# A weight loaded in three pieces, and the last transposes of a GLA and MLP-mixer kernel moved from TensorE to the DMA crossbar

## The chip, the cores and the metric

The kernel runs on one core of one Trainium2 chip. The metric is the device time of one execution in microseconds (us). The core has five engines that run their own instruction streams side by side: TensorE (matrix multiplies and transposes; PE in the profile, its weight loads PEld), VectorE (DVE), ScalarE (ACT), GpSimd (POOL) and SyncE (SP). SP computes nothing here; its queue issues every DMA of the kernel. The 16 DMA engines that move the data are shared by all transfers.

## The reference

Two stages follow each other, for four batches of 768 tokens. The first is a gated linear attention with 8 heads of 48, the second an MLP mixer over 384 channels.

```
for t in range(S):                                  # 768 tokens, per batch and head
    state = alpha[t] * state + outer(k[t], v[t])    # 48 x 48
    y[t] = q[t] @ state
x = y as [batch, token, 8 * 48]

h  = relu(x.T @ w_tok1) @ w_tok2                    # mixes tokens, 768 -> 256 -> 768
u  = x + h.T
h2 = relu(u @ w_ch1) @ w_ch2                        # mixes channels, 384 -> 1536 -> 384
out = u + h2
```

All inputs and the output are float32 in DRAM; the kernel multiplies in bf16.

## The kernel before

**Tiling.** A batch is cut into six chunks of 128 tokens, numbered through all batches (chunk 18 is the first of batch 3). The recurrence over tokens becomes matrix products inside a chunk and a 48 x 48 state per head handed from chunk to chunk.

**One chunk of attention.** Four loads bring alpha, k, q, v (`load`). ACT takes the logarithm of alpha (`la`, L243), TensorE sums it over the tokens (`cum`, L352), ACT exponentiates the sums with either sign (`ek`, `eq`, L256 and L258). POOL multiplies k and q by them (`pkk`, `pkq`, L275, one 128 x 384 product each; for batch 0 the q product is on DVE) and casts v (`vb`, L282). Keys and queries must then have channels on the partitions: TensorE transposes both in pieces of 64 x 64 into two PSUM banks (`tr`, through `row_tiles`, L289), and ACT or DVE copies the two banks to SBUF (`tp`, L297, into `tkq`). From there come the chunk's score matrix (`gt`, L387), its masking (`gm`, L309, DVE), the state (`state`, `st`, `ss`) and the output (`y`, then `x`, L333). The chunks of batches 0 and part of 1 are worked off in pairs by `paired_chunks`, with the same steps.

**The mixer of one batch.** `tok1` (L602) and `ht` (relu) mix the tokens down, `tok2` (L651) mixes them up again, and DVE adds x to give u (`u`, L657, one per chunk). u is transposed as well: `utp` (L667, again `row_tiles`) handles three chunks at a time (part 0 is chunks 0 to 2, part 1 chunks 3 to 5 of the batch) and `ut` (L669) copies two banks to SBUF. Batch 0 gets its transposed u by other matmuls (`mixed`, `xt` and `uT`). Then `ch1` (L691) has 24 groups of three matmuls, one for each of 12 blocks of 128 hidden channels and each half of the tokens; a group for half 0 reads only part 0 of the transposed u. ACT or DVE applies the relu (`rt`). `ch2` (L715) multiplies back, in three groups of four matmuls for each chunk (batch 3's last chunk in two column ranges), DVE adds u (`o`, L728), and SP stores the result (`out`, L731).

**Weights.** `weight` (L735) loads each weight in pieces into a staging tile and casts it to bf16 there. The first channel weight (`m0`, `m1`, 384 x 768 each) comes through the staging tile `rt_late`; each piece has three casts of 128 x 768 (the `cast` of L756). `ch1` finds the piece of a block by its column (`divmod(mc * 128, WP)`).

**Order.** Nothing is scheduled at run time. The calls of `g.add` number the operations, and the string `ORDER` lists these numbers in the order in which they are emitted; each engine works off its own operations in that order and waits where an input or a buffer isn't ready. A letter behind a number picks the engine (A, D, P), the digits behind a point the PSUM banks. An item `f2` is a fill: a matmul of zeros into bank 2 (L792) that keeps TensorE running where it would wait. The costs at `g.add` (`{"PE": 0.25}`, `dma=`) belong to the planner that wrote the order; at run time they do nothing but name the engine.

All loads and stores stand in one sequence on SP's queue. Input tiles have eight slots, so loads run ahead of the work by up to eight chunks. The last load is chunk 23's v; only stores come behind it.

Of the kernel before, what the change touches and what calls it, by code (L numbers as in the profile page):

```python
# [25 lines left out]
0 1 f0 2 f0 f0 f0 f0 f0 3 f0 f0 f0 f0 f0 4 28 f0 29 f0 f0 30.0 5 31.1 32 f2 f2 38 6 f2 35 f2 33 f2 f2 f2 39 f2 34 f2  # L26
36 40 f2 43.2 41 7 f3 66 47.3 f4 65 48 44 49A 50D f4 67.4 46A 45D 68.5 69 f6 51.67 75 72 54.01 8 70 52 f3 f3 76 f3 73
f3 77 f3 80.3 78 f2 9 84.2 56 f6 85 105 81 71 f6 104 87D f6 f6 10 86A f6 f6 83D 106.6 82A 55 107.5 108 53 91.14 11 114
88.23 92 f0 42P 37A f0 f0 109 90 f0 58.07 115 89 57.13 60A 93 f2 116 12 f2 f2 59 f2 f2 f2 112 f2 111 63 61 117 14
123.2 64A f0 62 f0 124 74A 79P 119.0 110 16 120 125D 126A f4 94.41 122A 121D 18 96 127.57 97 130.36 95.20 128 113A  # L30
118P 100 132 98 102 133.4 99A 20 131 13P f5 103A 169.5 101 163.6 24 166.2 f3 15P 129 141.3 135 142.0 143 136 134.17
17P 137 139 145 138D 147 140A 144 146 259 148 150 149 151 19D 152 172.4 178.1 162A 161D 175.7 f0 173 176 174A 167 177D
260 164 168A 170 22D 21P 165A 179 f0 171A 23D f0 261 f0 180A f0 189.0 201.3 190A 195.4 262 202A 181.7 27D 25P 196A
185.2 26D 182A 153 193.6 186A 211.5 264 194D 223.1 263 212D 227.0 224A 265.3 228A 266.4 155 267 217.7 273 270 207.2
274 209.6 268 300 208D 218A 276 213.5 210D 215.1 214A 269 187.0 301 271 216A 203.4 188A 219.3 275 204A 302 225.2 220A
154D 199.7 272 226A 278.65 277 279 200A 303 221.1 280D 281A 156P 183.0 222A 282 283 184A 292.43 284D 285A 197.2 304
294 286.71 157 305 198D 289.05 205.6 287 306.4 288 206A 159 191.2 308 291 307.7 309 311 239.6 296 314 343 290 315
# [41 lines left out]
class Graph:  # L79
# [5 lines left out]
    def add(self, name, costs, emit, reads=(), writes=(), prio=0, dma=None, new=(), tail=0.0, rows=False, loose=False, n=0, late=0.0):  # L85
        self.ops.append(Op(costs, emit, new))
        return self.ops[-1]
# [6 lines left out]
def kernel(  # L94
# [12 lines left out]
    nc = tc.nc  # L107
    B, H, S, D = q.shape
    C = 128
# [725 lines left out]
```

## Time and profile before

| what | value |
|---|---|
| time, median of 3 runs | 174.1 us (174.01 to 174.3) |
| the profiled execution | 174.24 us |
| its span in the trace | 172.5 us |
| DMA, mean over the span | 30.20 MB, 175 GB/s |
| first matmul of ch1, batch 0 | 33.1 us |
| first matmul of ch1, batch 3 | 146.3 us |

A row of a group reads: line, engine, operation, output<-inputs by the program's names, shape, xcount, then the busy time in all and the mean of one in ns, then how long the engine sat idle just before and what ended that. A row of the chain or of the timeline begins with the start in the span and a length in us; in the timeline, rows of one kind that follow each other closely are merged and the counts added. A row of a stretch of time gives its bounds, its length and each engine's busy time with the number of instructions. Matmuls overlap in the pipeline: one of 128 x 384 is listed with 326 ns, and they follow each other every 0.16 us.

### The profile page before, as it was taken

Reading aid. Unit: us, or ns where it says so; the run is one execution under the profiler, and the core shown is the slowest. Engines: PE = TensorE matmul, PEld = TensorE weight load, DVE = VectorE, ACT = ScalarE, POOL = GpSimd, SP = SyncE. Lnnn points to the kernel's source line nnn. Section 1 sums busy time; section 2 is a strip of 40 time slices with the busy share of each in tenths; the row PEclk is TensorE's granted clock in tenths of the full one; section 3 lists DMA queues with packets and bytes.
Section 4 is the critical chain, followed back from the end, with each engine's and each line's share of the span. In section 5 each row is a group of like instructions: output and inputs, shape, how many; then the busy total and the mean of one; then the engine's idle time right before and its main releaser. Section 6 shows DMA issues by size and latency. Waiting matters only on the chain.

```text
span 172.5 us, 5143 instructions
## 1 busy us (share of the span) xinstructions
PE 166.5 (96%) x2099; PEld 106.8 (62%) x2099; DVE 102.0 (59%) x212; ACT 96.0 (56%) x206; POOL 72.3 (42%) x114
## 2 busy tenths in 40 slices
PE   7999979999999999999999999999999999999993
PEld 3566656665666567566666665666676656656562
DVE  3159977544653597689593727495988248132231
ACT  2577552699865655497887231699771112865000
POOL 7252542319485782944877111499941000000000
PEclk9999999999999999999999999999999999999999
DMA  5999999999998999999999999995000221100133
GB/s 134 261 261 265 232 335 398 309 234 337 256 307 168 205 254 219 225 170 198 165 204 151 196 219 223 211 210 92 4 4 0 79 104 50 46 4 0 46 115 113
DMA packets 86150, 30.20 MB, mean 175 GB/s; under 512 B 79600, under 2 KB 85104, under 8 KB 86128
## 3 DMA queue, kind: packets, MB, share of 16 engines
q1 hardware_dynamic: 86128, 29.89, 75.2%
q8 instruction: 16, 0.26, 0.7%
q14 instruction: 6, 0.05, 0.1%
HBM read 25.17 MB, written 4.72 MB: 173 GB/s over the span
## 4 chain that ended last, share of the span: by engine, by line
PE 78%; DVE 6%; POOL 4%; DMA 3%; issue 3%; ACT 2%; SPq 1%; DVEq 0%; POOLq 0%
PE bank L691 27%; PE bank L715 23%; PE bank L289 4%; PE bank L651 3%; DMA ina<-in_alpha_dram 3%; PE bank L602 3%; DVE gm L309 2%; PE bank L387 2%; PE bank L338 2%; PE bank L423 2%; POOL pkk L275 2%; PE bank L521 1%; PE bank L411 1%; PE bank L352 1%; SPq L205 1%
## 5 line engine op out<-in xcount | busy, mean ns | idle before, releaser
L691 PE MATMUL bank<-ut,wc 128*128 128x384 bf16 x288 | 51.1, 326 | 0.0
L691 PEld LDWEIGHTS <-wc 128*128 128x128 bf16 x288 | 26.6, 98 | 16.5
L275 POOL TENSOR_TENSOR pkk<-ink,ek 128x384 bf16<-128x384 f32 x24 | 24.3, 1022 | 17.7 <-ACT ek L256 14.9
L715 PE MATMUL bank<-wc,rt 128*128 128x384 bf16 x144 | 26.5, 326 | 0.0
L715 PE MATMUL bank<-wc,rt_late 128*128 128x384 bf16 (+2 forms) x156 | 25.1, 314 | 0.0
L728 DVE TENSOR_TENSOR o<-bank,x 128x384 f32<-128x384 f32 (+2 forms) x19 | 10.1, 536 | 18.2 <-PE bank L715 18.2
L589 ACT ACTIVATE rt<-bank 128x384 bf16<-128x384 f32 x33 | 16.3, 494 | 7.4 <-PE bank L691 7.0
L282 POOL CAST vb<-inv 128x384 bf16<-128x384 f32 x21 | 10.5, 506 | 22.3 <-DMA inv<-in_v_dram 17.6
L715 PEld LDWEIGHTS <-rt_late 128*128 128x128 bf16 x156 | 14.4, 98 | 8.2
L275 POOL TENSOR_TENSOR pkq<-inq,eq 128x384 bf16<-128x384 f32 x18 | 17.9, 1003 | 2.8 <-ACT eq L258 2.8
L589 ACT ACTIVATE rt_late<-bank 128x384 bf16<-128x384 f32 x33 | 16.1, 495 | 5.3 <-PE bank L691 5.3
L309 DVE TENSOR_TENSOR gm<-bank,u 128x512 bf16<-128x512 f32 x28 | 17.3, 682 | 2.8 <-PE bank L387 2.6
L243 ACT ACTIVATE la<-ina 128x384 bf16<-128x384 f32 x24 | 12.1, 526 | 10.8 <-DMA ina<-in_alpha_dram 10.8
L715 PEld LDWEIGHTS <-rt 128*128 128x128 bf16 x144 | 13.2, 98 | 7.7
L792 PE MATMUL bank<-zeros 128*128 128x384 bf16 x61 | 15.1, 372 | 1.4 <-DVE la L192 1.2
L591 DVE TENSOR_SCALAR rt_late<-bank 128x384 bf16<-128x384 f32 x15 | 8.3, 554 | 10.0 <-PE bank L691 8.3
L309 DVE TENSOR_TENSOR gm<-bank,pmask 128x512 bf16<-128x512 f32 x20 | 12.7, 682 | 1.4 <-PE bank L521 1.3
L256 ACT ACTIVATE ek<-bank 128x384 f32<-128x384 f32 x24 | 11.4, 498 | 3.5 <-PE bank L355 2.0
L333 ACT CAST x<-bank 128x384 bf16<-128x384 f32 x16 | 7.3, 483 | 10.6 <-PE bank L338 9.4
L322 POOL TENSOR_TENSOR ss<-st,al 128x384 bf16<-128x384 f32 x12 | 10.0, 832 | 7.4 <-DVE st L319 5.4
L591 DVE TENSOR_SCALAR rt<-bank 128x384 bf16<-128x384 f32 x15 | 7.9, 554 | 5.3 <-PE bank L691 5.3
L297 ACT COPY tkq<-bank 128x512 bf16<-128x512 bf16 x17 | 9.3, 602 | 2.8 <-PE bank L289 2.7
(118 smaller groups left out, 237.3 us busy)
## 6 DMA issues: line engine op xcount, KB each, us to landing
out_dram<-o SPq DMA_DIRECT2D x23, 192.0 KB, 2.6
ina<-in_alpha_dram SPq DMA_DIRECT2D x14, 192.0 KB, 4.3
ink<-in_k_dram SPq DMA_DIRECT2D x14, 192.0 KB, 4.6
inq<-in_q_dram SPq DMA_DIRECT2D x14, 192.0 KB, 4.5
inv<-in_v_dram SPq DMA_DIRECT2D x14, 192.0 KB, 4.4
rt_late<-in_moe_w_ch_dram SPq DMA_DIRECT2D x2, 1152.0 KB, 10.1
rt_late<-in_moe_w_ch_dram SPq DMA_DIRECT2D x4, 576.0 KB, 7.1
ina<-in_alpha_dram SPq DMA_DIRECT2D x5, 384.0 KB, 6.3
```

Source lines behind the costliest of these rows:

```text
L243: g.add("la", {"ACT": 0.43}, lambda e: act.activation(la[:, :, 0:D], t, AF.Ln), key, [u["la"][1]], pr + 5)
L256: g.add("ek", {"ACT": 0.38}, lambda e: act.activation(ek, banks[bank.place][:, 0:HD], AF.Exp, scale=-1.0), [bank], [kek], pr + 4)
L275: lambda e, dst=dst, src=src, ex=ex: {"POOL": gps, "DVE": dve}[e].tensor_tensor(dst[:, :, 0:D], src, ex().rearrange("p (h d) -> p h d", h= ...
L282: lambda e: evict[e](vb, src), ksrc, [u["vb"][1]], pr + 4)
L309: g.add("gm", {"DVE": 0.60}, lambda e: dve.tensor_tensor(gm, banks[bank.place].rearrange("p (j t) -> p j t", j=4), wide(mask, [[0, 4], lis ...
L322: g.add("ss", {"POOL": 0.79}, lambda e: gps.tensor_tensor(ss, st.rearrange("p (h d) -> p h d", h=H), wide(al, [[1, 8], [0, D]]), ALU.mult) ...
L589: act.activation(dst, src, AF.Relu)
L591: dve.tensor_scalar_max(dst, src, 0.0)
L691: pe.matmul(banks[bank.place][:, 0:HD], lhsT=wc1[wp][:, kc, off : off + 128], rhs=ut_t[b % 2][:, kc, cs], start=(kc == 0), stop=(kc == NM ...
L715: pe.matmul(banks[bank.place][:, 0 : hi - lo], lhsT=rt_t[(b * NDC + mc) % NRT][:, i * 128 : i * 128 + 128], rhs=wc2[:, mc, lo:hi], start=( ...
L728: g.add("o", {"DVE": 0.09 + 0.38 * width}, lambda e, i=i, bank=bank, o=o, lo=lo, hi=hi: dve.tensor_tensor(o[:, lo:hi], banks[bank.place][: ...
L792: pe.matmul(banks[place][:, 0:HD], lhsT=zeros[:, 0:128], rhs=zeros, start=True, stop=True, skip_group_check=True)
```

## The change

Four edits and a new order.

1. The first channel weight is loaded in three pieces of 512 columns (`NWP = 3`, a third load `m2`), each with three casts of 128 x 512.
2. For batch 3 (`UTD`) the transposes of u by TensorE and the copies out of PSUM go. In their place SP issues one transposing DMA for each part, from SBUF to SBUF, 128 x 1152.
3. For chunks 21, 22 and 23 (`TRD`) the same is done for keys and queries: two transposing DMAs of 128 x 512 for each chunk.
4. For this the tiles of x are three to one tile, and the transposed u is laid out as chunk, channel block, token, where it was channel block, token; ch1 reads its right-hand side as three runs of 128.

The flag `TOT` is off, so the code that it guards isn't used.

```
-LOADS = "a0 k0 q0 a1 k1 q1 a2 v0 k2 q2 v1 v2 t0 t1 t2 t3 m0 m1"
+LOADS = "a0 k0 q0 a1 k1 q1 a2 v0 k2 q2 v1 v2 t0 t1 t2 t3 m0 m1 m2"
+UTD, TRD, TOT = (3,), (21, 22, 23), False
...
-    x_t = many("x", NX, [128, HD])
+    x_all = many("x", 4, [128, 3, HD])
+    x_t = [x_all[n // 3][:, n % 3, :] for n in range(NX)]
...
-    ut_t = many("ut", 2, [128, NM, S])
+    ut_t = many("ut", 2, [128, NCH, NM, C])
...
-    NWP = 2
+    NWP = 3
...
     def s_transpose(n, dst, key, prio):
         u, tb = units[n], [Bank(), Bank()]
+        if n in TRD:
+            for i, w in enumerate("kq"):
+                src, ksrc = u["p" + w]
+                g.add("trd", {"SP": 1.2}, lambda e, i=i, src=src: nc.sync.dma_start_transpose(
+                    dst[:, i], src.rearrange("p h d -> p (h d)")), [ksrc], [(*key, i)], prio, dma=0.8)
+            return
...
+            if b in UTD:
+                x = x_all[(n0 + mine[0]) % NX // 3]
+                g.add("utd", {"SP": 1.3}, lambda e, x=x, cs=cs: nc.sync.dma_start_transpose(
+                    ut[:, cs].rearrange("p i j t -> p (i j) t"), x.rearrange("p i d -> p (i d)")), ku,
+                    [("ut", b % 2, j, part, h) for j in range(NM) for h in range(2)], 1000 * b + 170, dma=1.6)
+                continue
...
-                              rhs=ut_t[b % 2][:, kc, cs], start=(kc == 0), stop=(kc == NM - 1),
+                              rhs=ut_t[b % 2][:, ti, kc, :], start=(kc == 0), stop=(kc == NM - 1),
```

The order string is new from end to end. It holds 956 operations (959 before: one load and three casts more, one transpose and two copies replaced by two DMAs for each of three chunks, one and two by one DMA for each part of u) and 58 fills (61 before). Decoded into names, these are TensorE's own operations around the moved transposes, first from the first cum of batch 3's last chunks to gt 23 (`ch1 2 6.1` is batch 2, block 6, half 1; `ch2 2 0p1` is batch 2, chunk 0, group 1):

```
before: cum 20, cum 18, cum 21, ch1 2 3.1, cum 19, ch1 2 2.0, 10.1, 0.1, 5.0, 4.1, 9.0, state 19, state 18, cum 22,
        ch1 2 6.1, 7.1, 5.1, 7.0, 6.0, 1.0, 10.0, cum 23, state 20, tr 20, tr 19, tr 18, ch1 2 4.0, 8.0, 11.0, tr 21,
        gt 20, gt 19, gt 18, ch1 2 9.1, 3.0, 1.1, state 22, ch1 2 0.0, y 18, gt 21, ch1 2 2.1, y 19, y 20, tr 23,
        tr 22, state 21, y 21, ch1 2 8.1, ch2 2 5p0, gt 23
after:  cum 19, ch2 1 4p2, cum 18, cum 20, cum 21, ch1 2 6.1, 11.1, state 19, ch1 2 10.0, 9.0, state 18, cum 22,
        ch1 2 6.0, 11.0, 3.1, tr 18, tr 19, ch1 2 3.0, 4.0, state 20, gt 18, gt 19, ch1 2 0.0, 7.1, cum 23,
        ch1 2 1.0, state 21, y 18, ch1 2 2.0, 1.1, y 19, tr 20, ch1 2 5.0, 2.1, 9.1, 8.0, 4.1, state 22,
        ch1 2 7.0, 5.1, 10.1, gt 20, gt 21, ch1 2 0.1, 8.1, ch2 2 0p0, y 20, ch2 2 5p0, 5p1, gt 23
```

and from batch 3's token mixing to its first ch1:

```
before: tok2 0, 5, 2, 1, 3, 4, ch2 2 0p1, 0p2, 3p1, utp 1, utp 0, ch2 2 3p2, ch1 3 8.1, 4.1, 1.0, 8.0
        DVE: u 0, 5, 2, 1, 4, 3, o (chunk 0)
after:  tok2 2, 0, 1, 3, 5, 4, ch2 2 1p0, 1p1, 1p2, 2p1, 2p2, 4p0, 4p1, 4p2, ch1 3 5.0, 6.0, 9.0, 11.0, 1.1
        DVE: o (chunk 0), o (chunk 3), u 2, 0, 1, 5, 4, 3, o (chunk 1)
```

SP's queue after the last load:

```
before: out 2 1, 5, 2, 4, 0, 3, out 3 1, 4, 3, 0, 2, 5
after:  trd 21 k, 21 q, 22 q, 22 k, 23 k, 23 q, out 2 5, 0, 3, utd part 0, utd part 1, out 2 1, 2, 4, out 3 2, 3, 0, 4, 1, 5
```

POOL works in the new order on pkk 19, pkk 18, pkq 18, pkq 19, pkk 20, pkq 20, pkk 21, pkq 21, pkq 22, pkk 22, pkk 23, pkq 23 (before: pkk 20, 18, 19, pkq 18, 19, 20, 21, pkk 21, 23, 22, pkq 23, 22). Batch 0's first groups of ch1 are 0.0, 3.0, 1.1, 7.0, 4.0, 4.1, 9.0 in the new order (4.0, 4.1, 1.1, 0.0, 2.0, 0.1, 9.0 before), with no fill between uT and the first of them (four before). In the copies of the transposed keys and queries of batch 0, DVE has one of the six `tpq` and four of the `tpk` (three and three before).

More of the change, by code (lines that the diff above doesn't have):

```diff
@@ L31 @@
[L31 to L35, printed above, removed]
@@ L67 @@
+922 935 939 923 940 943 924 927 925 944 928 945 946.0 929 947 930 948 951.5 952 949 953 950 954 955
 """
@@ L83, in __init__, with add @@
         self.ops = []
-    def add(self, name, costs, emit, reads=(), writes=(), prio=0, dma=None, new=(), tail=0.0, rows=False, loose=False, n=0, late=0.0):
+    def add(self, name, costs, emit, reads=(), writes=(), prio=0, dma=None, new=(), tail=0.0, rows=False, loose=False, n=0, late=0.0, banks=(), gates=()):
         self.ops.append(Op(costs, emit, new))
```

111 lines of the change are left out of this document (61 added, 50 removed).

## The prediction

> **What bounds the kernel now.** I read the page first: the busy times, the slices and the split of the chain of waits.
>
> ```profile
> span 172.5 us, 5143 instructions
> ...
> PE 166.5 (96%) x2099; PEld 106.8 (62%) x2099; DVE 102.0 (59%) x212; ACT 96.0 (56%) x206; POOL 72.3 (42%) x114
> ...
> DMA  5999999999998999999999999995000221100133
> ...
> PE 78%; DVE 6%; POOL 4%; DMA 3%; issue 3%; ACT 2%; SPq 1%; DVEq 0%; POOLq 0%
> ```
>
> TensorE is busy for 96% of the span and carries 78% of the chain; the DMA engines are full until about 118 us and nearly empty after that. A share of a whole span hides the stages, so I next asked for the busy time of each engine (columns PE, PEld, DVE, ACT, POOL; then clock, DMA share, GB/s) in four stretches: up to the first channel matmul, batches 0 to 2, batch 3's attention and token mixing, batch 3's channel mixing.
>
> ```profile
> 0.00:33.00 33.00, 30.14 (x444) 19.63 (x445) 20.53 (x58) 17.93 (x39) 13.92 (x30) 1.00 1.07 276
> 33.00:110.00 77.00, 76.61 (x1037) 48.66 (x1036) 48.91 (x91) 50.20 (x108) 41.20 (x59) 1.00 1.05 220
> 110.00:146.00 36.00, 36.00 (x466) 23.65 (x465) 25.00 (x49) 18.56 (x42) 17.20 (x25) 1.00 0.31 73
> 146.00:172.50 26.50, 23.74 (x158) 14.84 (x156) 7.60 (x15) 9.30 (x19) 0.00 (x0) 1.00 0.16 56
> ```
>
> From 33 us to the last matmul TensorE pauses for 0.39 us in 77 and for nothing in the next 36; the granted clock is 1.00 throughout. So from 33 us on, a microsecond of matmul or transpose that is taken out moves the end by a microsecond, unless something that TensorE needs then comes too late. Before 33 us the busy time contains the fill matmuls, which stand where it waits; there a shorter wait is what pays.
>
> ```profile
> L792 PE MATMUL bank<-zeros 128*128 128x384 bf16 x61 | 15.1, 372 | 1.4 <-DVE la L192 1.2
> ```
>
> Last, the chain in order of time (start, length, what) around the parts that the change touches.
>
> ```profile
> 121.27 0.34 PE bank L289 x16
> ...
> 126.37 0.57 PE bank L289 x32
> ...
> 141.03 1.95 PE bank L651 x12
> 142.98 1.95 PE bank L715 x12
> 144.93 0.63 PE bank L289 x36
> ...
> 146.31 11.70 PE bank L691 x72
> ```
>
> L289 is the transposing helper. The x16 at 121.27 are chunk 21's keys and queries, the x32 at 126.37 chunks 23's and 22's, the x36 at 144.93 batch 3's u. All of them lie on the chain, in a stretch without a pause.
>
> **The change part by part.** *Transposes taken from TensorE.* They cost 0.34 + 0.57 + 0.63 = 1.54 us of the chain, and all of it goes. With them go six copies of tkq and four of ut on ACT and DVE:
>
> ```profile
> L297 ACT COPY tkq<-bank 128x512 bf16<-128x512 bf16 x17 | 9.3, 602 | 2.8 <-PE bank L289 2.7
> L669 ACT COPY ut<-bank 128x576 bf16<-128x576 bf16 x6 | 3.7, 649 | 7.4 <-PE bank L289 7.4
> ```
>
> At these durations (the share on DVE costs less) that is at most 6 x 0.60 + 4 x 0.65 = 6.2 us of two engines. ACT and DVE are busy 18.56 and 25.00 of 36 us there and hold nothing up, so I count it as nothing; it only loosens.
>
> *Transposes given to SP's queue.* Six transfers of 128 KB (128 x 512 of two bytes) and two of 288 KB (128 x 1152). No crossbar transpose stands in the trace, so its time is bounded by plain transfers (size, median us from issue to landing):
>
> ```profile
> out_dram<-o SPq DMA_DIRECT2D x23, 192.0 KB, 2.6
> ink<-in_k_dram SPq DMA_DIRECT2D x14, 192.0 KB, 4.6
> ...
> ink<-in_k_dram SPq DMA_DIRECT2D x5, 384.0 KB, 7.7
> ...
> out_dram<-o SPq DMA_DIRECT2D x1, 128.0 KB, 1.7
> out_dram<-o SPq DMA_DIRECT2D x1, 64.0 KB, 1.5
> ```
>
> Below: 1.7 us for 128 KB and, along the slope from 64 to 192 KB (1.1 us in 128 KB), 3.4 us for 288 KB. Above: the loads in a full queue, 4.6 us for a chunk's transfer and 7.7 us for one of u. I take the lower values, since the slices show the engines almost idle where the transposes run (after the last load).
>
> How much cover do they have? For u: in the trace the six u additions run behind the token matmuls that start at 141.03:
>
> ```profile
> 141.39 2.88 DVE L657 TENSOR_TENSOR x<-bank,x 128x384 bf16<-128x384 f32 x6 [0.42 <-PE bank L651]
> ...
> L728 DVE TENSOR_TENSOR o<-bank,x 128x384 f32<-128x384 f32 x17 | 9.4, 557 | 17.2 <-PE bank L715 17.2
> ```
>
> So one comes every 0.49 us. In the new order an o addition of batch 2 (0.56 us) stands ahead of them on DVE, which puts their start at about 0.6 us after the first tok2 (0.36 before); u of chunks 2, 0, 1 is complete at +2.1 us, of 5, 4, 3 at +3.5. TensorE meanwhile has its own six tok2 (1.95) and eight groups of ch2 at 0.65 (1.95 for three): its first ch1 of batch 3 stands at +7.15, and four such groups, each 11.70/24 = 0.49, read part 0 alone, so part 1 is needed at +9.1. The cover is 5.05 us and 5.6 us, against 3.4. Behind each waiting transpose on SP stand only the other one and three stores of batch 2; the o tiles that these free are written again only in batch 3's ch2, behind the 11.70 us of its ch1. For the chunks:
>
> ```profile
> 109.82 0.33 PE L352 MATMUL bank<-la,u 128*128 128x384 bf16 x1
> ...
> 110.11 0.51 POOL L282 CAST vb<-inv 128x384 bf16<-128x384 f32 x1 [4.72 <-PE bank L715]
> 110.89 1.96 POOL L275 TENSOR_TENSOR pkk<-ink,ek 128x384 bf16<-128x384 f32 x2 [0.27 <-ACT ek L256]
> ...
> 123.26 1.96 POOL L275 TENSOR_TENSOR pkq<-inq,eq 128x384 bf16<-128x384 f32 x2
> ...
> 128.66 0.62 PE L387 MATMUL bank<-tkq 48*128 48x128 bf16 x16
> ...
> 115.11 1.34 SPq L205 DMA_DIRECT2D inv<-in_v_dram  x1
> ```
>
> POOL makes the twelve products of chunks 18 to 23 from 110.89 to 125.22, 14.3 us, starting 1.1 us after the stage's first cum at 109.82. In the new order the same products end with chunk 23's queries, so at +15.4 us after its first cum. TensorE took 18.84 us from that cum to gt 23 (the L387 at 128.66). Between the same two, the new order has one group of ch1 (0.49) and three of ch2 (1.95) more, and the transposes of three chunks (0.34 + 0.57) and one y (under 0.4) less: gt 23 moves to +20.0 us. That leaves 4.6 us for the last of the six transposes, against 1.7. They follow products that come about 1 us apart, and the last load before them on SP was issued at 115.11, so SP has time for each. I count no stall. What would be lost if a cover is short is in the rivals.
>
> *The first channel weight in three pieces.* Bytes are the same, and SP issues one load more, before the loads of batch 1. The start of the channel stage in the chain, the first casts of the two old pieces, and batch 0's copies on DVE:
>
> ```profile
> 29.62 0.50 ACT ht L589
> ...
> 30.49 1.95 PE bank L634 x12
> 32.44 0.65 PE bank L792 x4
> 33.09 4.39 PE bank L691 x27
> ...
> 30.73 0.83 POOL L756 CAST wc<-rt_late 128x768 bf16<-128x768 f32 x1 [3.63 <-DMA rt_late<-in_moe_w_ch_dram]
> ...
> 33.71 1.22 POOL L756 CAST wc<-rt_late 128x768 bf16<-128x768 f32 x1 [2.15 <-DMA rt_late<-in_moe_w_ch_dram]
> ...
> L481 DVE COPY tq<-bank 128x512 bf16<-128x512 bf16 x3 | 2.0, 683 | 1.4 <-ACT tq L481 1.4
> ...
> L479 DVE COPY tk<-bank 128x512 bf16<-128x512 bf16 x3 | 1.2, 416 | 1.1 <-ACT tk L479 1.1
> ```
>
> The pieces landed at 30.7 and 33.7, 2.98 us for 1152 KB; thirds would land at about 29.7, 31.7 and 33.7. The four fills (0.65 us, 0.16 each) between the token matmuls and ch1 cover the casts of piece 0 and vanish when it lands a microsecond sooner: the new order has none there. Its ch1 needs piece 1 at the fourth group, 1.5 us in (about 34.1), and piece 2 at the seventh, 2.9 us in (about 35.5); a cast of 512 columns is about two thirds of the 0.83 to 1.02 us of a POOL cast, so both are ready with 0.5 us or more to spare. Over the whole order the fills go from 61 to 58, 3 x 0.16 = 0.5 us. I take 0.5 us for the start. Bounds: a gain of 1.6 us (the 0.65, and 0.95 us less of copies on DVE while it works off batch 0's attention: two large ones fewer, one small one more), or a loss of 0.6 us if the wait before ch1 returns in another place.
>
> *The layouts of ut and x.* ch1 now reads three runs of 128 columns in place of one of 384. cum reads eight runs of 48 columns already and is no slower (327 against 326 ns), so nothing:
>
> ```profile
> L352 PE MATMUL bank<-la,u 128*128 128x384 bf16 x14 | 4.5, 327 | 0.0
> L691 PE MATMUL bank<-ut,wc 128*128 128x384 bf16 x288 | 51.1, 326 | 0.0
> ```
>
> *Sum.* The profiled execution took 174.24 us, 1.74 more than its span; 174.24 - 1.54 - 0.5 = **172.2 us**. The median of the three runs is 174.1, so the profile lies 0.1 us above it, less than matters here.
>
> **The rivals.** *(a) The loads set the pace.* The DMA engines are full until 118 us. The cast at 110.11 is chunk 21's v; the releaser named had long been done, so it waited for its load, and the products could start only 0.27 us later than they could anyway. If TensorE arrives earlier and the data doesn't, the gain at the start is lost and POOL's 14.3 us may also set when chunk 23 is ready. Only the u transposes are then sure: 174.24 - 0.63 = 173.6; with all transposes saved, 172.7; I put it at 173.2. Against it: the new order puts one store less ahead of that load.
>
> *(b) The crossbar is late.* Part 0 of u decides: a landing later than 5.05 us after its u stalls ch1. At the 7.7 us of the full-queue row it lands at +9.8, a stall of 2.65 us, and the time is 174.9; if the two share one stream, so that part 1 lands another 3.4 us later, at +13.2 against +9.1 + 2.65, it adds 1.45, and the time is 176.3. I put it between, at 175.6, slower than before. The chunks' transposes would at 4.6 us just hold. For it: no row shows this operation, and the full-queue loads move short runs (48 values of four bytes), as a transpose by rows of 128 two-byte values would. Against it: the queue is empty by then.
>
> *(c) The crossbar works block by block*, each block of 128 x 128 at the fixed price of the smallest store, 1.5 us. A chunk's transfer is then 6 us, six in a row 36 us from about +9.3 (chunk 21's keys are POOL's seventh product), against gt 23 at +20.0: a stall of 25.3 us. The two u transposes at 13.5 us each, the second behind the first, land at +15.6 and +29.1, against +7.15 and +9.1 + 8.45, and add 8.45 and 11.55 us. The time would be 172.2 + 45.3 = 217.5. Nothing in the trace speaks for it, as 128 KB land in 1.7 us where 64 KB take 1.5. The Trainium skill does: VectorE: DVE Perf Modes, section The three transpose paths, gives 1309 ns for a 128 x 128 block on the DMA path against 390 on TensorE, and taken once per block that would be an estimated 11.8 us for each part of u. Its Advanced Engine Details and Errata, section X-Bar Transpose (TRN2), says the contrary, that such transfers are as fast as ordinary ones; by that the rows of plain transfers hold. No run here shows either.
>
> *(d) The new order gives back what the transposes save*: nearly all of its 956 operations have moved, and one wait like the 0.5 us for ht at 29.62, three or four times, is enough. The time stays at 174.2. Against it: the work between is the same and was gapless.
>
> **How the numbers follow.** Forecast 0.54, (a) 0.14, (b) 0.18, (c) 0.05, (d) 0.09. The forecast's own range is 171.1 to 173.3 (the start gaining 1.6, or losing 0.6). The range of 171.0 to 175.6 takes in (a), (d) and the nearer half of (b), and leaves out (c), the farther half and a start better than thought. Differences under 0.2% (0.35 us) can't be told from none here. Faster: forecast and (a) less 0.01 for (a)'s far end, 0.67; same: most of (d), 0.07; slower: (b), (c), the rest of (d), 0.26.
>
> **What would show it.** Right: L289 falls by 84 transposes; no pause of TensorE before gt 21 to 23 and before batch 3's first ch1; the u transposes land in under 5 us from their issue; the first ch1 starts near 32.6, and batch 3's ch1 still takes 11.7 us. Wrong: a wait of L387 or of ch1 on a transposing transfer (b, c); idle POOL at about 109 to 111 on a load, followed by waits on TensorE (a); new pauses or fills between 33 and 110 us (d); a first ch1 at or after 33.1.

## The result and the profile after

The changed kernel takes 173.09 us (median of 6 runs, 172.37 to 173.86) against 174.14 us before; the ratio is 0.9939 with a 95% interval of 0.9912 to 0.9966. The change made the kernel faster by 0.3 to 0.9%, about 1.05 us; the forecast was 172.2 us, a gain of twice that. The profiled execution took 172.97 us with a span of 171.0 us (before: 174.24 and 172.5), so the span is 1.5 us shorter, and 0.23 us of that is lost outside the span. A ratio leaves out single executions more than 1.5% above the fastest of their kernel: none here, but three or four of the twelve of m2_later, v13_first and alpha_early below, whose ratios are lower for it.

The line numbers moved: the transposing helper is L290, cum L359, gt L402, the state L426, y L438, x L340, the masking gm L316, tok2 L666, the u addition L672, uT's matmuls L649, ch1 L712, ch2 L736 (batch 0's part with u L732), batch 0's transposes of keys and queries L487, the casts of the first channel weight L777, those of the other weights L783, the fills L813, the loads L206, the transposing DMAs L308 (keys and queries) and L682 (u). The first view is the busy time in stretches (columns PE, PEld, DVE, ACT, POOL; clock, DMA share, GB/s), in the same stretches as before.

```profile
0.00:33.00 33.00, 31.18 (x448) 19.82 (x449) 20.52 (x59) 20.42 (x43) 13.70 (x30) 1.00 1.04 272
33.00:110.00 77.00, 75.70 (x1034) 48.73 (x1033) 47.97 (x91) 49.55 (x108) 41.27 (x60) 1.00 1.03 218
110.00:146.00 36.00, 36.00 (x387) 23.14 (x386) 23.00 (x44) 17.29 (x41) 16.77 (x25) 1.00 0.56 124
```

Between 33 and 110 us TensorE now pauses for 1.30 us where it paused for 0.39. In the 36 us from 110 to 146, in which the moved transposes ran, it pauses for nothing, as before. The chain of waits shows both ends of batch 3's mixing and the start of batch 0's.

```profile
30.00 1.95 PE bank L649 x12
31.95 3.09 PE bank L712 x19
35.03 0.04 issue
35.08 1.96 PE bank L712 x11
...
137.62 1.95 PE bank L666 x12
139.57 5.20 PE bank L736 x32
144.77 5.36 PE bank L712 x33
```

The first ch1 of batch 0 stands at 31.95 (33.09 before), with a gap of 0.05 us after 19 of its matmuls; that of batch 3 at 144.77 (146.31). From tok2's end at 139.57 eight groups of ch2 run into ch1 without a gap; no row of L290 stands between. With these points the profiled span divides into three parts:

| part | before | after | difference |
|---|---|---|---|
| start to first ch1 of batch 0 | 33.09 | 31.95 | -1.14 |
| to first ch1 of batch 3 | 113.22 | 112.82 | -0.40 |
| to the end | 26.19 | 26.23 | +0.04 |

The middle part should have lost the 1.54 us of transposes. It gained 0.91 us of pauses (1.30 less 0.39), which leaves 0.63; 0.40 was measured. Of the difference 0.1 us is visible: the transposes of chunks 18 to 20 took 0.81 us in one block before, and take 0.57 and 0.34 in two now. No row explains the other 0.13.

The view of the DMA issues (median us from issue to landing) and SP's queue in time show the new transfers:

```profile
out_dram<-o SPq DMA_DIRECT2D x1, 128.0 KB, 1.9
...
tkq<-pkk SPq DMA_TRANSPOSE x3, 2.5
tkq<-pkq SPq DMA_TRANSPOSE x3, 3.1
ut<-x SPq DMA_TRANSPOSE x2, 3.3
```

```profile
115.52 0.72 SPq L206 DMA_DIRECT2D inq<-in_q_dram  x1
...
118.58 1.30 SPq L308 DMA_TRANSPOSE tkq<-pkk  x1
120.33 3.16 SPq L308 DMA_TRANSPOSE tkq<-pkq  x2
123.58 2.58 SPq L308 DMA_TRANSPOSE tkq<-pkk  x2
126.27 1.21 SPq L308 DMA_TRANSPOSE tkq<-pkq  x1
...
139.64 2.73 SPq L682 DMA_TRANSPOSE ut<-x  x2
```

A transfer of 288 KB lands 3.3 us after its issue. The six of 128 KB land after 2.4 to 3.7 us; the rows give the medians of the keys' three and the queries' three, and the slowest are the first two of the queries (3.7 and 3.1 us). SP itself is occupied for 1.2 to 1.3 us with each of the eight, once for 1.8 (the last four plain loads ahead of them took 0.7 to 1.5), so that six in a row, whose data come 1.0 to 1.7 us apart, form a queue. The last product, chunk 23's queries, ends on POOL at 124.72, and gt 23 stands in the chain at 129.34; SP issues the transfer between them only at 126.27, and it lands 2.4 us later.

```profile
123.73 0.99 POOL L276 TENSOR_TENSOR pkq<-inq,eq 128x384 bf16<-128x384 f32 x1
```

```profile
129.34 0.55 PE bank L402 x16
```

What ended TensorE's waits is in the view of waits (us in total, times, longest). One row is left out: 1.2 us of a fill for `la`, which was there before.

```profile
PE bank L487 <- DVE pkq L276: 0.4, 1, 0.4
PE bank L426 <- POOL vb L283: 0.3, 1, 0.3
PE bank L290 <- DVE x L672: 0.2, 1, 0.2
PE bank L732 <- DVE x L340: 0.2, 1, 0.2
PE bank L438 <- DVE gm L316: 0.2, 1, 0.2
```

The same view of the kernel before has, beside that fill and 0.2 us for `ht`, only this row; it has none of the lower four:

```profile
PE bank L521 <- DVE tk L479: 1.4, 2, 1.0
```

The lower four stand between 50 and 75 us. The first of them has a load behind it, as the chain of the changed kernel says (the page's shares by engine, then the pieces in time):

```profile
PE 77%; DMA 9%; SPq 7%; DVE 3%; ACT 1%; issue 1%; POOL 0%; DVEq 0%; ACTq 0%
```

```profile
68.94 0.28 SPq L752
...
69.26 4.93 DMA inv<-in_v_dram
...
74.25 0.51 POOL vb L283
...
74.80 0.33 PE bank L426 x4
```

The state of chunk 13 (L426) waits for v, which SP issues only at 69.26, behind a store. Before, the chain went through DMA for 3% of the span and through SP's queue for 1%; but nearly all of SP's 7% and 7.5 of the DMA's 16 us lie in the first 20 us. What is new between 60 and 75 us are two loads, of 3.6 and 4.9 us.

### The profile page after: what moved, and what is told of

Same layout as the page of the kernel before. It is cut to its first block, busy times and chain, and to the rows that moved or that the text cites. A ratio compares the mean times of both kernels' runs of the same rounds, so it can differ in the third digit from the quotient of the medians.

```text
span 171.0 us, 4970 instructions
## 1 busy us (share of the span) xinstructions
PE 165.1 (97%) x2012; PEld 105.6 (62%) x2012; DVE 97.2 (57%) x204; ACT 96.3 (56%) x207; POOL 71.7 (42%) x114
## 4 chain that ended last, share of the span: by engine, by line
PE 77%; DMA 9%; SPq 7%; DVE 3%; ACT 1%; issue 1%; POOL 0%; DVEq 0%; ACTq 0%
PE bank L712 28%; PE bank L736 25%; SPq L206 6%; DMA inq<-in_q_dram 4%; DMA inv<-in_v_dram 3%; PE bank L617 3%; PE bank L666 2%; DMA ina<-in_alpha_dram 2%; PE bank L402 2%; PE bank L345 2%; PE bank L438 2%; DVE gm L316 2%; PE bank L290 2%; PE bank L597 1%; PE bank L649 1%; PE bank L359 1%
## 5 line engine op out<-in xcount | busy, mean ns | idle before, releaser
L712 PE MATMUL bank<-ut,wc 128*128 128x384 bf16 x288 | 50.8, 326 | 0.0
L712 PEld LDWEIGHTS <-wc 128*128 128x128 bf16 x288 | 26.7, 98 | 16.9 <-POOL wc L777 0.4
L276 POOL TENSOR_TENSOR pkk<-ink,ek 128x384 bf16<-128x384 f32 x24 | 23.7, 997 | 20.6 <-ACT ek L257 18.2
L736 PE MATMUL bank<-wc,rt 128*128 128x384 bf16 x144 | 26.4, 326 | 0.0
L736 PE MATMUL bank<-wc,rt_late 128*128 128x384 bf16 (+2 forms) x156 | 24.8, 314 | 0.0
L604 ACT ACTIVATE rt_late<-bank 128x384 bf16<-128x384 f32 x36 | 17.5, 497 | 11.0 <-PE bank L712 10.8
L316 DVE TENSOR_TENSOR gm<-bank,u 128x512 bf16<-128x512 f32 x28 | 17.8, 682 | 3.4 <-PE bank L402 2.5
L283 POOL CAST vb<-inv 128x384 bf16<-128x384 f32 x21 | 11.1, 530 | 20.3 <-DMA inv<-in_v_dram 20.3
L736 PEld LDWEIGHTS <-rt_late 128*128 128x128 bf16 x156 | 14.5, 98 | 8.3
L736 PEld LDWEIGHTS <-rt 128*128 128x128 bf16 x144 | 13.2, 98 | 7.7
L604 ACT ACTIVATE rt<-bank 128x384 bf16<-128x384 f32 x32 | 15.6, 501 | 3.2 <-PE bank L712 3.2
L813 PE MATMUL bank<-zeros 128*128 128x384 bf16 x58 | 14.0, 365 | 1.2 <-DVE la L193 1.2
L316 DVE TENSOR_TENSOR gm<-bank,pmask 128x512 bf16<-128x512 f32 x20 | 12.7, 683 | 3.0 <-PE bank L536 3.0
L606 DVE TENSOR_SCALAR rt_late<-bank 128x384 bf16<-128x384 f32 x12 | 6.5, 555 | 11.5 <-PE bank L712 11.5
L606 DVE TENSOR_SCALAR rt<-bank 128x384 bf16<-128x384 f32 x16 | 8.7, 554 | 7.1 <-PE bank L712 6.9
L340 ACT CAST x<-bank 128x384 bf16<-128x384 f32 x14 | 6.6, 481 | 10.4 <-PE bank L345 8.5
L259 ACT ACTIVATE eq<-bank 128x388 f32<-128x388 f32 (+2 forms) x18 | 9.2, 518 | 0.0
```

What stands on the lines that cost most here:

```text
L276: lambda e, dst=dst, src=src, ex=ex: {"POOL": gps, "DVE": dve}[e].tensor_tensor(dst[:, :, 0:D], src, ex().rearrange("p (h d) -> p h d", h= ...
L283: lambda e: evict[e](vb, src), ksrc, [u["vb"][1]], pr + 4)
L316: g.add("gm", {"DVE": 0.60}, lambda e: dve.tensor_tensor(gm, banks[bank.place].rearrange("p (j t) -> p j t", j=4), wide(mask, [[0, 4], lis ...
L604: act.activation(dst, src, AF.Relu)
L606: dve.tensor_scalar_max(dst, src, 0.0)
L712: pe.matmul(banks[bank.place][:, 0:HD], lhsT=wc1[wp][:, kc, off : off + 128], rhs=ut_t[b % 2][:, ti, kc, :], start=(kc == 0), stop=(kc == ...
```

## The experiments

Each kernel is the changed kernel with one edit; edits of the order are given in the names of the operations. All ratios are to the kernel before, measured beside it; the changed kernel's own is 0.9939 (0.9912 to 0.9966), and 0.1% is 0.17 us. The changed kernel was not measured again beside the others, so a difference between its ratio and another carries both intervals, together about 0.6 to 0.7 us either way. Profiled times are of one execution, which can lie far from the median: late_start's is the slowest of its twelve (174.92 us, median 173.79), and those of alpha_early (173.52, median 175.33), no_trd and both light kernels are the fastest of theirs.

| kernel | ratio (95%) | span | first ch1, batch 0 | chunk 13's state | first ch1, batch 3 |
|---|---|---|---|---|---|
| changed | 0.9939 (0.9912 to 0.9966) | 171.0 | 31.95 | 74.80 | 144.77 |
| no_trd | 1.0066 (1.0041 to 1.0092) | 173.0 | 31.83 | 73.97 | 146.68 |
| no_utd | 0.9993 (0.9963 to 1.0022) | 173.2 | 31.90 | 75.57 | 146.86 |
| no_cross | 1.0048 (1.0015 to 1.0081) | 173.7 | 32.06 | 74.45 | 147.49 |
| no_cover | 1.0071 (1.0045 to 1.0098) | 173.8 | 32.01 | 75.26 | 143.46 |
| two_pieces | 0.9973 (0.9952 to 0.9994) | 172.2 | 31.86 | 75.94 | 145.98 |
| m2_later | 0.9917 (0.9879 to 0.9955) | 171.9 | 31.90 | 75.14 | 145.48 |
| late_start | 0.9949 (0.9920 to 0.9979) | 172.9 | 32.87 | 75.62 | 146.72 |
| v13_first | 0.9931 (0.9892 to 0.9970) | 171.5 | 31.91 | 75.04 | 145.03 |
| light | 0.9914 (0.9885 to 0.9943) | 170.3 | 31.91 | 73.99 | 143.97 |
| light_late | 0.9921 (0.9896 to 0.9946) | 170.9 | 32.81 | 74.74 | 144.72 |
| alpha_early | 1.0006 (0.9973 to 1.0040) | 171.6 | 31.87 | 75.45 | 145.42 |
| four_chunks | 0.9949 (0.9914 to 0.9985) | 173.3 | 32.00 | 76.53 | 146.94 |

(In no_cover groups of ch2 stand behind ch1, so its last column is not comparable.)

### What the transposes are worth

**no_trd**: keys and queries of chunks 21 to 23 go back to TensorE, with two copies each.

```
-TRD = (21, 22, 23)
+TRD = ()
+tr 21 behind ch1 2 5.0, tr 22 behind ch1 2 8.1, tr 23 behind ch2 2 0p0, each with two copies (DVE, ACT)
```

> The changed kernel with the keys and queries of chunks 21, 22 and 23 transposed by TensorE again. Theory 'TensorE bounds batch 3': the three transposes come back on the chain, 0.34 + 0.57 = 0.91 us, so about 174.0 us (changed kernel 173.1 median), batch 3's first ch1 at about 145.7 in the span (144.77 in the changed kernel). Rival 'the loads and POOL set the pace of batch 3': the transposes fit into time that TensorE would wait anyway, 173.1 us and a first ch1 near 144.8.

The ratio is 1.0066, 1.3% or 2.2 us above the changed kernel, give or take 0.7. The transposes' own 0.91 us is less than half of it. Two waits of TensorE are new:

```profile
PE bank L438 <- ACT tkq L298: 0.7, 1, 0.7
PE bank L736 <- DVE tkq L298: 0.5, 1, 0.5
```

A ch2 group and a y wait for a copy out of PSUM. Their first matmuls don't read what is copied: they write a bank that was given to the transposes just ahead, bank 1 to chunk 22's and bank 3 to chunk 23's.

**no_utd**: batch 3's u goes back to TensorE, with four copies.

```
-UTD = (3,)
+UTD = ()
+utp 0 behind ch2 2 2p1, utp 1 behind ch2 2 2p2, each with two copies (ACT, DVE)
```

> The changed kernel with batch 3's u transposed by TensorE again, between the ch2 groups of batch 2. Theory 'TensorE bounds batch 3': plus 0.63 us, 173.7 us, first ch1 of batch 3 at about 145.4. Rival 'nothing was gained by u's transposes': 173.1 us.

0.9993 is 0.5% or 0.9 us above the changed kernel, give or take 0.7. Batch 3's own stretch has the two transposes (0.41 and 0.44 us in the chain) and a wait of 0.3 us for a bank that an o addition held. This execution also had pauses of 1.5 us for `la` and a cast at 53 to 61 us, where nothing had been edited.

**no_cross**: both parts back on TensorE, with other banks than in no_trd and no_utd; one group of ch2 stands later for it, and banks 4 and 7 change places from there on.

```
-UTD, TRD = (3,), (21, 22, 23)
+UTD, TRD = (), ()
+tr 21 behind ch1 2 2.1, tr 22 behind gt 21, tr 23 behind y 20, utp 0 behind ch2 2 1p2, utp 1 behind ch2 2 2p1
+ch2 2 0p0 directly ahead of ch2 2 0p1 (ahead of y 20 in the changed kernel)
```

> All transposes are on TensorE again with their copies out of PSUM, in the changed kernel's order and with banks that no other operation needs at the same time; the weight stays in three pieces. Theory (TensorE has no pause from 75 us on, so each transpose costs its length): 173.1 + 1.54 = 174.6 us, batch 3's first ch1 1.5 us later than in the changed kernel, and 0.6 us of it between batch 3's last tok2 and its first ch1. Rival (the crossbar's transposes cost time of their own, by DMA traffic or waits, that their removal gives back): 173.8 us or less.

1.0048 is 1.1% or 1.9 us above the changed kernel, and the kernel is slower than the one before. With both intervals that is 1.9 us, give or take 0.7: it holds the theory's 1.54 us and excludes the rival's 0.7 us or less. Between cum 23 (118.4 in both) and batch 3's first ch1 they differ by 2.7 us. Transposes account for 1.76 of it (three of 0.34 us, two of 0.37 between groups of ch2: cut into single blocks they take more than the 1.54 of the old order's). The rest is hardly a wait: in these 29.1 us TensorE pauses for 0.14, as another group of ch1 covers most of a copy that a bank waits for. But a group of ch1 or ch2 right behind a block of transposes takes 0.1 us more than another (0.76 for 0.65 in a group of ch2), here behind four of the five blocks. About 0.4 us stay unexplained. Two of the blocks:

```profile
143.29 0.37 PE bank L290 x18
143.66 0.76 PE bank L736 x4
144.42 0.37 PE bank L290 x18
```

So the transposes are worth their length and a little more. The bank waits of no_trd are a matter of the banks that were chosen there: with others all five blocks cost no more, by the ratios, than its three. As put back here, the third piece and the new order without the crossbar are a loss of 0.5%.

**no_cover**: five groups of ch2, with the additions and stores that follow them, stand behind batch 3's sixth group of ch1 in place of ahead of the first.

```
-ch2 2 1p0, 1p1, 1p2, 2p1, 2p2, 4p0, 4p1, 4p2, ch1 3 5.0, 6.0, 9.0, 11.0, 1.1, 6.1
+ch2 2 1p0, 1p1, 1p2, ch1 3 5.0, 6.0, 9.0, 11.0, 1.1, 6.1, ch2 2 2p1, 2p2, 4p0, 4p1, 4p2
```

> The changed kernel with five groups of ch2 of batch 2 (3.25 us) moved from ahead of batch 3's first ch1 to behind its sixth group: the same work, less cover for u's crossbar transposes. They land 3.3 us from issue in the changed kernel, the first is issued about 2.0 us after tok2 starts, and ch1 would now stand at 3.9 us after it. Theory 'the crossbar's time is hidden by that cover alone': a stall of about 1.4 us before batch 3's first ch1, 174.5 us. Rival 'it is hidden anyway': 173.1 us.

The wait comes, 1.5 us in the view of waits, and the chain runs through the transfer:

```profile
140.00 0.11 DVE x L672
140.11 3.31 DMA ut<-x
...
143.46 3.10 PE bank L712 x18
```

The last u addition of the part ends at 140.11, the transfer takes 3.31 us, and ch1 starts 0.05 us later. With three groups in place of eight the cover is 5 x 0.65 = 3.25 us shorter and the stall 1.47 us long: in the changed kernel 1.8 us of cover are left over. By the ratios (four executions here) the kernel is 2.3 us above the changed one, 0.8 us more than the stall. The trace has two other delays: chunk 13's state stands 0.46 us later, and ch1 waits 0.2 us for an o addition behind the moved groups. What the rest is isn't known.

### What the third piece is worth

**two_pieces**: the weight is loaded in two pieces of 768 columns as before, in the new order.

```
-LOADS = "... m0 m1 m2"
+LOADS = "... m0 m1"
-NWP = 3
+NWP = 2
```

> The changed kernel with the first channel weight in two pieces of 768 columns, in the same order. My prediction said that the smaller first piece lets ch1 of batch 0 start sooner. Theory 'size': the first ch1 falls back by about 0.6 us, from 31.95 to about 32.6, or the groups behind it wait for the second piece, and the time is about 173.7 us. Rival 'order': piece 0 lands near 30.7, its casts end by 31.7, before the ut copies let ch1 start at 31.95; the first ch1 stays within 0.2 us and the time at 173.1 to 173.3; the start's gain then comes from the new order of batch 0's attention.

Its first ch1 stands at 31.86, no later than with three pieces. The casts show why; first the changed kernel, then this one, then the kernel before.

```profile
29.57 0.43 DVE L777 CAST wc<-rt_late 128x512 bf16<-128x512 f32 x1
29.60 0.87 POOL L777 CAST wc<-rt_late 128x512 bf16<-128x512 f32 x1 [1.15 <-DMA rt_late<-in_moe_w_ch_dram]
29.61 0.61 ACT L777 CAST wc<-rt_late 128x512 bf16<-128x512 f32 x1
...
34.15 0.87 POOL L777 CAST wc<-rt_late 128x512 bf16<-128x512 f32 x1 [1.48 <-DMA rt_late<-in_moe_w_ch_dram]
35.08 1.58 PEld L712 LDWEIGHTS <-wc 128*128 128x128 bf16 x11 [0.38 <-POOL wc L777]
```

```profile
30.26 0.83 ACT L777 CAST wc<-rt_late 128x768 bf16<-128x768 f32 x1 [0.63 <-DMA rt_late<-in_moe_w_ch_dram]
30.26 0.56 DVE L777 CAST wc<-rt_late 128x768 bf16<-128x768 f32 x1 [0.73 <-DMA rt_late<-in_moe_w_ch_dram]
30.29 1.21 POOL L777 CAST wc<-rt_late 128x768 bf16<-128x768 f32 x1 [2.10 <-DMA rt_late<-in_moe_w_ch_dram]
...
34.17 0.10 PEld L712 LDWEIGHTS <-wc 128*128 128x128 bf16 x1 [1.23 <-ACT wc L777]
```

```profile
31.65 1.02 DVE L756 CAST wc<-rt_late 128x768 bf16<-128x768 f32 x2
```

In the new order ACT, DVE and POOL each cast one part of the first piece side by side, and even a piece of 768 columns is ready at 31.50. Before, DVE cast two parts one behind the other and was done at 32.67; the four fills covered that. So the start doesn't need the smaller pieces. What they bring comes later. With 768 columns the weight loads of ch1 wait 1.23 us for the second piece; with 512 they wait 0.38 us for the third, nearly all of it hidden, since weight loads run ahead of the matmuls (the gap of 0.05 us at 35.03). From 33 to 50 us TensorE is busy for 15.96 us of 17 with two pieces and for 16.95 with three, so the third piece is worth 1.0 us there in this order, and 0.34% or 0.6 us, give or take 0.6, by the ratios. The order was made for three pieces: its fourth group of ch1, 7.0, lies in the second piece either way. The kernel before takes its first group of the second of two pieces, 9.0, as the seventh, 2.9 us in. An order for two pieces with 7.0 at that place would reach it at an estimated 34.8 us (31.86 and six groups of 0.49), when the last cast of the second piece (33.31 to 34.53) is done; it wasn't tried, so what the third piece is worth against the best order for two isn't shown.

**m2_later**: a group that reads the second piece is taken ahead of the first that reads the third.

```
-ch1 0 9.0, 5.1
+ch1 0 5.1, 9.0
```

> Batch 0's group of ch1 5.1, whose columns lie in the second piece, stands ahead of 9.0, the first that reads the third piece, so that TensorE should not wait for the third piece's cast (0.4 us near 35 us in the changed kernel). Theory (loads of batch 1 set the pace until 75 us): the pause at 35 us goes, 0.4 us of pauses come in at 50 to 75 us, the time stays at 173.1 within 0.2 us. Rival (TensorE sets the pace): 172.7 us.

The wait near 35 us isn't there, but it cost TensorE only the gap of 0.05 us: both sides of the expectation had read the 0.38 us of the weight loads as a pause of the matmuls, and there was nothing of that size to tell apart. Nor was it the edit that removed it: in no_trd, no_utd, no_cross and no_cover, whose order is unchanged here, TensorE is busy for 17.00 us of the 17 as well, because the third piece's casts begin between 33.5 and 33.9 us where they began at 34.12; and in four_chunks, which has the same edit, weight loads wait again, as the pieces land later. The ratio, 0.9917, can't be told from 0.9939. The run shows something else. From 50 to 60 us, where nothing was edited, TensorE is busy for 9.16 us, against 9.80 in the changed kernel:

```profile
50.00:60.00 10.00, 9.16 (x163) 5.67 (x162) 5.12 (x10) 4.62 (x8) 6.46 (x11) 1.00 0.89 191
```

The pauses there differ from one traced execution to the next by as much as the effects that were sought.

### Where the gain of the start goes

**light**: seven eighths of q and v of chunks 10 to 17 are left out, so the output is not the reference's.

```
+hs = slice(0, 1 if w in "qv" and n < 18 else H)
-load_input(t, src[b, :, ts : ts + C, :] ...)
+load_input(t[:, hs], src[b, hs, ts : ts + C, :] ...)
```

> The loads of q and v of chunks 10 to 17 bring one head of the eight in place of all (7/8 of 192 KB less for each of 16 loads, 2.7 MB of 30); the other heads are computed from what the slot held before. All else as in the changed kernel. Theory (the pauses of TensorE for la, vb and casts at 50 to 80 us come from late loads): they go, and only the three waits on DVE (x L340, gm L316, x L672, 0.2 us each) stay; chunk 13's state, at 74.8 us in the changed kernel, stands near 74.1, the time falls by 0.5 to 0.8 us to 172.3 to 172.6, and its spread between executions gets smaller. Rival (these pauses come from the order of the work on the engines): the waits stay, 173.1 us.

All waits behind loads are gone, and only the three on DVE are left between 33 and 110 us (each of 0.2 us; L291, L733 and L439 in this kernel). The whole stretch, in place of the changed kernel's 75.70 us and 1.03:

```profile
33.00:110.00 77.00, 76.18 (x1049) 49.20 (x1047) 48.31 (x91) 50.12 (x110) 41.61 (x61) 1.00 0.85 191
```

The DMA engines are no longer full, chunk 13's state stands at 73.99, 0.8 us sooner, and the span is 0.7 us shorter. One trace alone would say little, as no_trd has that state at 73.97 with full loads. But TensorE is busy for 76.18 us of this stretch in light_late too, and for 74.6 to 76.0 in all eleven traces of the new order with full loads. So the pauses beyond the three do come from the loads, about 0.5 of the changed kernel's 1.30 us. By the ratio the kernel gains 0.25%, 0.4 us, with intervals that overlap. The spread between executions did not shrink (172.3 to 173.7 us): what causes it isn't these waits alone.

**late_start** and **light_late**: six fills ahead of batch 0's first ch1, with full and with light loads.

```
+f1 f1 f1 f1 f1 f1
 ch1 0 0.0
```

> Six fills (0.16 us each, 0.98 us) stand ahead of batch 0's first group of ch1; all else as in the changed kernel. Theory (the loads of batch 1 set the pace between 50 and 75 us, so a late start is made good there): first ch1 near 32.9 us, the pauses of TensorE between 50 and 75 us shrink by about as much as the start is late, batch 3's first ch1 and the time move by less than 0.3 us (173.1 to 173.4). Rival (TensorE sets the pace, the pauses there have other causes): batch 3's first ch1 and the time move by the whole 0.98 us, to 174.1.

> The light loads of the run before, and six fills (0.98 us) ahead of batch 0's first ch1. Theory (the loads give back what the start gains or loses): with the loads out of the way the start counts in full, so the time is that of the light loads plus 0.8 to 1.0 us, about 173.3 us, where the same fills with full loads cost 0.2 us. Rival (fills cost the same whatever the loads): light loads plus 0.2 us.

In both kernels ch1 starts 0.9 us later, and in both the traces still show 0.8 us of it at chunk 13's state (75.62 against 74.80, and 74.74 against 73.99); with light loads 0.75 us of it also reach batch 3's first ch1. So the traces agree with the theory on the light loads. With full loads they can't tell: late_start's trace is the slowest of its twelve executions, and in the ten other traces with full loads and the early start that state stands anywhere from 73.97 to 76.53. The times speak the other way on the light loads: by the ratios the fills cost 0.10% (0.2 us) with full loads and 0.07% with light ones, where the whole 0.98 us would be 0.56%. The intervals, of 0.3% on either side for each ratio, make that unlikely but don't exclude it. The traced executions and the timed ones don't agree here, and the theory is not shown.

**v13_first**: the load that the chain shows late is issued ahead of the store.

```
-out 0 3, load v 13
+load v 13, out 0 3
```

> In SP's queue the load of chunk 13's v stands ahead of the store of batch 0's chunk 3; nothing else differs. Theory (the loads are late in batch 1 and 2, and a store ahead of them makes them later): TensorE's wait for chunk 13's state near 74 us shrinks by 0.3 to 0.6 us, and the time falls to 172.5 to 172.8 us. Rival (the wait there has another cause, or the time that it gives back is lost at the next load): no wait of TensorE at 74 us goes, or the time stays at 173.1 us.

The wait of L426 is gone, and others stand earlier:

```profile
PE bank L359 <- ACT la L244: 0.8, 1, 0.8
...
PE bank L736 <- DVE wc L783: 0.2, 1, 0.2
```

Both end between 54 and 60 us, before the edited place, and the wait for la there has 0.7 us in no_cover as well, whose loads are unchanged: this one trace doesn't say that the edit moved a wait. The ratio, 0.9931, is that of the changed kernel.

**alpha_early**: seven loads of alpha stand earlier.

```
-k 1, q 1, v 1, n2, n3, a 10, k 10, q 10, v 10, a 11, k 11, q 11, ...
+k 1, a 10, q 1, v 1, n2, n3, k 10, a 11, q 10, v 10, k 11, a 12, q 11, ...
```

> In SP's queue each alpha load of chunks 10 to 16 stands two to four loads earlier than in the changed kernel (ahead of the q load of the chunk before), the k, q and v loads that it passes one place later; the bytes are the same. Theory (loads are late, and alpha is the first thing that a chunk needs): TensorE no longer waits for la, and the time falls by 0.2 to 0.6 us to 172.5 to 172.9 us. Rival (all loads are equally late, so the wait moves to vb or the products): other waits on loaded data of the same total take their place, 173.1 us.

TensorE doesn't wait for la, as it didn't in the changed kernel's trace either. It waits for the cast of a weight piece and again for v:

```profile
PE bank L736 <- ACT wc L783: 0.9, 1, 0.9
PE bank L426 <- POOL vb L283: 0.4, 1, 0.4
```

The cast's load now comes one place later, but no_utd, with unchanged loads, has the same wait of 0.8 us. The ratio rises to 1.0006, 0.7% or 1.2 us above the changed kernel, which is clear of the intervals; the traced execution is the fastest of the twelve, with a span only 0.6 us above the changed kernel's, and doesn't show where the 1.2 us go. The theory fell; that all loads there are equally late, as the rival says, fits but isn't shown.

### One step further

**four_chunks**: chunk 20 through the crossbar too, and the edit of m2_later.

```
-TRD = (21, 22, 23)
+TRD = (20, 21, 22, 23)
-ch1 0 9.0, 5.1
+ch1 0 5.1, 9.0
```

> Two edits that aim at a faster kernel: chunk 20's keys and queries also go through the crossbar from SP's queue (32 transposing matmuls and two copies less), and batch 0's group of ch1 5.1 stands ahead of 9.0. All else as in the changed kernel. Theory (transposes cost TensorE their length, the crossbar is hidden): 0.34 us less for the transposes and up to 0.4 us for the wait near 35 us, 172.4 to 172.8 us. Rival (the cover of the last chunk's transposes is used up, since SP issues one every 1.2 to 1.6 us and they land 2.5 to 3 us after their issue): gt 23 waits 0.3 us or more for its queries, the time stays at 173.1 us or above.

The rival holds. SP's queue in time:

```profile
126.27 2.57 SPq L308 DMA_TRANSPOSE tkq<-pkk  x2
128.94 1.21 SPq L308 DMA_TRANSPOSE tkq<-pkq  x1
```

and TensorE's timeline:

```profile
131.44 0.62 PE L402 MATMUL bank<-tkq 48*128 48x128 bf16 x16 [0.82 <-DMA tkq<-pkq]
```

The last product ends at 126.47 in this execution's chain, its transfer is issued at 128.94 and lands at 131.4. The 0.82 us in the row are gt 23's wait. The ratio is no better than the changed kernel's. None of the versions tried is clearly faster than the changed one: light reaches 0.9914 by leaving out data, and m2_later's 0.9917 lies inside the changed kernel's interval.

## Why the prediction was right, and where it was off

**Direction and range** held: 173.1 us lies within 171.0 to 175.6, and the kernel is faster. The forecast's sum was too good by 0.9 us. For the profiled executions, 1.27 us apart, it closes like this: 1.54 us for the transposes and 1.14 for the start, less 0.91 of new pauses, 0.10 for the transposes of chunks 18 to 20, 0.13 that no row explains, 0.04 behind batch 3's first ch1 and 0.23 outside the span. That the total came so near is in part luck: the start gave 0.64 us more than its term, for another reason than the one forecast, and hid most of the pauses that weren't.

**The transposes (1.54 us, of the chain).** Right in mechanism: the rows are gone, TensorE has no pause in the stretch, and ch1 of batch 3 runs without a gap. Put back in no_cross, they cost 1.9 us by the ratio, give or take 0.7, and 2.7 us in the trace: their length, and 0.1 us for the return to ch1 or ch2 behind each block, which the term of 1.54 left out. Counting the copies as nothing ("it only loosens") left out the banks: two PSUM banks for each chunk and part are freed as well. That needn't cost much, as no_cross shows, but with the banks of no_trd it cost 1.2 us.

**The crossbar's price.** The estimate of 3.4 us for u was right (3.3 us), and its cover of 5.05 us also (no_cover leaves 1.8 us over, and 5.05 less 3.3 is 1.75). For the chunks 1.7 us was too low, 2.4 to 3.7 us were measured, and "SP has time for each" was wrong: at 1.2 to 1.8 us for each issue the queue ran behind POOL. The last transfer's cover was 4.6 us as forecast (from 124.72 to gt 23 at 129.34), but 1.55 us of it passed before the issue at 126.27; of the other 3.07 the landing took 2.4, and that just held. Gt 23 waited 0.3 us in one kernel that differs only in batch 0 (m2_later, where one issue took 2.7 us), and 0.8 us with two transfers more. Rival (b) fell for u, and was near for the chunks.

**Rival (c), block by block**, fell. A part of u holds nine blocks of 128 x 128 and lands in 3.3 us. By the 1309 ns that the Trainium skill gives for one block on the DMA path (VectorE: DVE Perf Modes, section The three transpose paths), taken for each block, it would have been an estimated 11.8 us. The Trainium skill's page Advanced Engine Details and Errata, section X-Bar Transpose (TRN2), says that transpose DMAs are as fast as regular ones. The rows come near that: 128 KB take 2.4 to 3.7 us here where a plain store of 128 KB takes 1.9.

**The start (0.5 us).** Mis-sized, and for a wrong reason. It gained 1.14 us: 0.65 us of fills, all four, and 0.49 us because uT starts at 30.00 instead of 30.49. Ahead of that TensorE's 1.4 us of waiting for `tk` has become 0.4 us for `pkq`; how much of that counts wasn't tested. That lies inside the bound of 1.6. But "vanish when it lands a microsecond sooner" is refuted by two_pieces: its pieces are the old ones, and it starts as early. With the casts side by side on three engines the fills aren't needed. The claim that piece 2 has "0.5 us or more to spare" failed too: the start came 0.65 us sooner than forecast (31.95 against 32.6), the third piece's last cast began at 34.15, and TensorE came to it 0.05 us too early in this execution, though not in most others of this order. That in this order the third piece is worth 1.0 us in the trace, not for the start but for the second piece behind it, stood nowhere in the prediction.

**What the sum left out.** 0.91 us of new pauses between 33 and 110 us. Of the 1.30 us that are there now, 0.6 us are the three waits on DVE. They stand in every kernel of this order, also with light loads: they belong to the new order, and are rival (d) at a third of its price. Of the other 0.7 us in this execution about 0.5 are waiting behind loads, rival (a)'s mechanism, but from 50 to 75 us in place of 110; at 109.7 POOL does wait 4.3 us for a load, and TensorE has no pause behind it. Light loads remove the 0.5, and neither of the two other orders of the loads does. It varies: chunk 13's state stands between 73.97 and 76.53 us in kernels whose work up to there is nearly the same, so one profile shows such a wait to no better than a microsecond.

**Still open.** By the times a start that is 0.9 us later costs 0.2 us, by the traces with light loads 0.75 us. So how much of the start's 1.14 us reaches the end isn't known, nor is the cause of the spread of 1.5 us between executions of the changed kernel. The 0.23 us outside the span are no chance: every execution of the changed kernel spends 1.9 to 2.1 us there and every one of the kernel before 1.7 to 1.8. No_trd, no_utd and no_cross are back at 1.65 to 1.8, but so, nearly, is two_pieces, which keeps all eight transposing DMAs; the cause isn't known.

## What to carry to other kernels

An operation that runs on an engine without pauses is worth its length, and the buffers that it holds can cost as much again: count the PSUM banks of a transpose before calling its copies free. A DMA that replaces it needs cover for three things, the landing, the issue on its queue, and every issue ahead of it there; the chain of the last one is what decides. When a stage is opened earlier and the loads behind it already fill the DMA engines, look there for new waits, and don't trust one profile with their size. And before a gain is put down to a smaller piece, try the old size in the new order, and an order made for the old size.

## What the runs showed of the hardware

A transposing DMA from SBUF to SBUF held SP's queue for 1.2 to 1.3 us per issue (once 1.8 us in the changed kernel, once 2.7 in m2_later), against 0.7 to 1.5 us for the last four plain loads ahead of it, and nearly the same for 128 KB as for 288 KB (1.31 and 1.32 us for the two of u). Its landing grows far less than the size: 2.4 to 3.7 us for 128 KB with a median of 2.5, 3.3 us for 288 KB.
